# Loading 80 of 128 partitions of the queries and keys, and values in one run a partition, in an attention kernel with two MLPs

## The chip, the cores and the metric

The kernel runs on one core of a Trainium2 chip. The metric is the device time of one execution in microseconds (us); less is better. The kernel before was run three times.

## What is computed

A causal block attention (4 batches, 8 heads, 576 positions, 64 values a head; all in float32), then two MLPs on the 2304 tokens of width 512, each with a hidden width of 2048.

```
def _attn_ref(q, k, v):
    scores = scale * np.matmul(q, k.transpose(0, 1, 3, 2))
    mask = block_i >= block_j                # blocks of 64 positions
    scores = np.where(mask, scores, -1000000000.0)
    attn = np.exp(scores - max); attn = attn / (sum + 1e-09)
    return np.matmul(attn, v)
...
    x = attn_out.transpose(0, 2, 1, 3).reshape(B * S, H * D)
    x = (np.maximum(x @ w_in, 0.0) ** 2) @ w_out             # first MLP
    return rational(x @ w_in2, a, b) @ w_out2                 # second MLP
```

## The kernel before

The work goes through three stages on the same engines. In the first one attention is computed head by head, and half of the first MLP's hidden units (`moe_a`) are woven between. Then come the other half of the first MLP (`yb`, `hb`) and the second MLP (`hc`, `yc`). In all of them TensorE multiplies, ScalarE (ACT) and VectorE (DVE) empty the accumulators, and GpSimd (POOL) does element-wise work from memory on chip.

Attention is done in *visits* (`Visit`, L172). Heads 0 to 7 are visited twice: visits 0 to 7 do the tiles 0 to 2 of their rows (`gis == (0, 1)`), visits 8 to 15 the tiles 3 and 4. From head 8 on one visit does a whole head. A visit consists of *slots*, and a slot i goes through the following chain: the scores S on TensorE (`emit_s`, L294, tiles `sy`, `sx`); the row maxima on DVE (`emit_max`, L315, `stat`); the exponentials with their sums on ACT (`emit_exp`, L328, tile `p`); transposes on TensorE (`emit_t`, L370, `tp`) and their copies into `pt_plain` by ACT (L388); the product with the values on TensorE (`emit_pv`, L429, `pv`), with the inverse sums spread by POOL (L344, `rb`), transposed (L436, `rows`), copied by ACT (L437, `xp`) and multiplied in by DVE (L438, `xp`). POOL turns the result into the operand `xt` of the first MLP (L451, L452), and a DMA stores it (L453).

Heads 0 to 9 are *plain* (`PLAIN = 10`): the scores are one product in float32. The host stacks the operand so that its first 64 partitions hold the head's 64 values, the next five hold marks that add the mask, and the other 59 hold zeros:

```
        out[:, 0:d_, pad:] = xt
        out[PLAIN:, d_:P, pad:] = xt[PLAIN:]
        for t in range(5):
            out[0:PLAIN, d_ + t, P * t:P * t + d_] = mark
```

Queries and keys are loaded by DMA with all 128 partitions (`load_qk`, L181, tiles `qr`, `kr`, two buffers under each of two tags in the first visits), and POOL scales the queries in place (`prep_qk`, L228), except those of visit 0. The values of two plain heads share one tile of 5 blocks of 128 columns, 64 of them for each head (`load_v`, L210), so that a load lands in pieces of 64 values. The heads 10 to 31 split both operands into two parts and need all 128 partitions; `make_two` (L200) copies partitions 64 to 127 of head 9's operands into constants for them.

Between all this, eight weight tiles `w_ai` of `moe_a` are converted (`Converter`, L81): a DMA loads `raw_ai` (512 KB, L93, three buffers), ACT and DVE make `cv_ai` of it (L117, and L118, L119, L121, L122), and the next call rounds it (ACT, L110) and subtracts (POOL, L111) into `w_ai`.

No order is written out by hand: the program lists the work, and a scheduler that estimates the duration of each instruction and transfer fixes one order for each engine when the kernel is built. On the chip an engine takes its instructions in this order, and each waits for what it needs. Scores have few accumulators (`sx` and `sy` one each, `mm` two), so a slot's scores wait until the exponentials four slots before have been read out. All of SP's transfers are issued in one order too, and at most eight are under way.

Of the kernel before, what the change touches and what calls it, by code (L numbers as in the profile page):

```python
# [8 lines left out]
F32 = mybir.dt.float32  # L9
# [8 lines left out]
P = 128  # L18
S = 576
SP = 640  # L20
D = 64
# [6 lines left out]
NB = 12  # L28
SCALE = 0.125
PLAIN = 10  # L30
SUBS = ((0, 320), (320, S))
SUB = 320
BLK = 512
# [11 lines left out]
def f(ap):  # L45
    return ap.bitcast(F32)
# [3 lines left out]
def attention_moe_moe(ctx: ExitStack, tc: tile.TileContext, q, k, v, wi1, wo1, wi2, wo2, a, b, out):  # L50
    nc = tc.nc
# [24 lines left out]
        name=nc.get_next_instruction_name(), act_func_set_id=EXP_LN_SET, ins=[], outs=[]))  # L76
# [59 lines left out]
    attn = tc.alloc_tile_pool(name="attn", bufs=1)  # L136
# [35 lines left out]
    class Visit:  # L172
        def __init__(self, n, hd, at, gis):
            self.n, self.hd, self.plain, self.at, self.gis = n, hd, hd < PLAIN, at, gis

            self.scale = SCALE if n == 0 else 1.0

            self.q0, self.q1 = (0, 3 * P) if gis == (0, 1) else (3 * P, SP) if gis == (2, 3) else (0, SP)
            self.k1 = SUB if gis == (0, 1) else S

    def load_qk(un, eng=nc.sync):  # L181
        if len(un.gis) == 2 and un.n % 4 > 1:

            un.qr = f(attn.tile([P, SP], F32R, tag="qh", name=f"qr{un.n}", bufs=2))
            un.kr = f(attn.tile([P, S], F32R, tag="kk", name=f"kr{un.n}", bufs=2))
        else:
            un.qr = attn.tile([P, SP], F32, tag="qr", name=f"qr{un.n}", bufs=2)
            un.kr = attn.tile([P, S], F32, tag="kr", name=f"kr{un.n}", bufs=2)

        cuts = ((0, 256, 0, 192), (256, un.q1, 192, un.k1)) if un.n == 0 else ((un.q0, un.q1, 0, un.k1),)  # L190
        for q0, q1, k0, k1 in cuts:
            nc.sync.dma_start(un.qr[:, q0:q1], q[un.hd][:, q0:q1])
            eng.dma_start(un.kr[:, k0:k1], k[un.hd][:, k0:k1])

# [13 lines left out]
    def load_v(un):  # L210
        src = v[un.hd].rearrange("p (c d) -> p c d", d=D)
        if un.plain:
            if un.hd % 2 == 0:
                un.vs = attn.tile([P, 5, P], F32, tag="vs", name=f"vs{un.n}", bufs=2)
            else:
                un.vs = units[un.n - 1].vs
            o = D * (un.hd % 2)
            nv = 3 if un.gis == (0, 1) else 5
            nc.sync.dma_start(un.vs[:, 0:nv, o:o + D], src[:, 0:nv])
        else:  # L220
            un.vr = attn.tile([P, 5, D], F32, tag="vr", name=f"vr{un.hd}", bufs=1)
            nc.sync.dma_start(un.vr, src)

    def prep_qk(un, step):
        if un.plain:
            if step == 0 and un.scale == 1.0:
                cols = un.qr[:, un.q0:un.q1]
                nc.gpsimd.tensor_scalar(cols, cols, SCALE, 0.0, op0=ALU.mult, op1=ALU.add)  # L228
            return
        if step == 0:  # L230
            hd = un.hd
            un.qh = attn.tile([P, SP], F32R, tag="qh", name=f"qh{hd}", bufs=2)
            un.kk = attn.tile([P, S], F32R, tag="kk", name=f"kk{hd}", bufs=2)
            nc.scalar.activation(un.qh, un.qr, AF.Copy, scale=SCALE)
            nc.scalar.activation(un.kk, un.kr, AF.Copy)
        else:
            un.q2, un.k2 = q_two[un.hd % 2], k_two[un.hd % 2]
            nc.vector.scalar_tensor_tensor(
                un.q2[0:D], un.qr[0:D], SCALE, f(un.qh[0:D]), op0=ALU.mult, op1=ALU.subtract)
            nc.gpsimd.tensor_tensor(un.kk[D:P], un.kr[D:P], f(un.kk[D:P]), op=ALU.subtract)  # L240
            nc.sync.dma_start(f(un.k2[0:D]), f(un.kk[0:D]))
# [24 lines left out]
    def emit_s(i):  # L266
        un, gi = slots[i]
        g = GROUPS[gi]

        upper = un.gis == (0, 1)  # L270
        if un.hd % 2 and gi == 0 if upper else gi % 2:
            ps = ps1.tile([P, 2, 512], F32, tag="sx", name=f"sx{i}")
            if gi != 3:
                ps = ps[:, 0, :]
        else:
            tag = "mm" if upper and gi == 1 else "sy"
            ps = ps1.tile([P, 512], F32, tag=tag, name=f"sy{i}", bufs=BANKS[tag])
        spsum[i] = ps
        for t in g:

            cols = slice(P * t, P * (t + 1))
            if un.plain:
                products = [(un.qr[:, cols], un.kr)]
            else:
                products = [(un.qh[:, cols], un.kk), (un.q2[:, cols], un.k2)]
            w_ = P * t + D
            if t == 4:
                parts = [(ps[:, 0, 0:HS], 0, HS), (ps[:, 1, 0:HS], HS, S)]
            else:
                o = D if t == 1 else 0  # L290
                parts = [(ps[:, o:o + w_], 0, w_)]
            for dst, lo, hi in parts:
                for z, (lhs, rhs) in enumerate(products):
                    last = nc.tensor.matmul(dst, lhs, rhs[:, lo:hi], start=z == 0, stop=z == len(products) - 1)  # L294
        marks.append(last)
# [62 lines left out]
    def emit_t(i):  # L358
        nonlocal pt
        un, gi = slots[i]  # L360
        g = GROUPS[gi]
        if un.hd == PLAIN and gi == 0:
            pt = attn.tile([P, 2, 3, SP], F32R, tag="pt", name="pt", bufs=1)
# [48 lines left out]
    def emit_pv(un, half):  # L412
        hd = un.hd
        b_, h = divmod(hd, H)
        hp, odd = divmod(h, 2)
        first, end = SUBS[half]
        n = end - first

        if un.plain and not odd:
            return  # L420
        if un.plain or not odd:
            xpair[hp, half] = attn.tile([P, SUB], F32, tag="xp", name=f"xp{hd}_{half}", bufs=3)
        xp = xpair[hp, half]
        ps = ps1.tile([P, 512], F32, tag="tp", name=f"pv{hd}_{half}", bufs=3)
        lo, hi = (0, D) if odd else (D, 0)
        if un.plain:
            for i, (c, src, dst, width) in enumerate(PV[half]):
                for n_, o in enumerate((0, D)):
                    nc.tensor.matmul(ps[o:o + D, dst:dst + width], un.vs[:, c, o:o + D],  # L429
                                     un.pt[:, n_, ROW[c], src:src + width],  # L430
                                     start=i == 0, stop=i == len(PV[half]) - 1)
            rb = spread.pop((hd, half))
            rows = ps1.tile([P, 512], F32, tag="tp", name=f"rows{hd}_{half}", bufs=3)
            lead = D if half == 0 else 0
            for at in range(rb.shape[1]):
                nc.tensor.transpose(rows[:, P * at:P * (at + 1)], rb[:, at], ident)  # L436
            nc.scalar.activation(xp[:, 0:n], rows[:, lead:lead + n], AF.Copy)  # L437
            nc.vector.tensor_tensor(xp[:, 0:n], ps[:, 0:n], xp[:, 0:n], op=ALU.mult)  # L438
        else:
            mm = [(z, *m) for z in range(2) for m in PV[half]]  # L440
            for i, (z, c, src, dst, width) in enumerate(mm):
                nc.tensor.matmul(ps[:, dst:dst + width], un.vs[:, c, :], un.pt[:, z, ROW[c], src:src + width],
                                 start=i == 0, stop=i == len(mm) - 1)
            tmp = attn.tile([P, SUB], F32, tag="tmp", name=f"tmp{hd}_{half}", bufs=2)
            nc.scalar.activation(tmp[hi:hi + D, 0:n], ps[lo:lo + D, 0:n], AF.Copy)
            nc.vector.tensor_tensor(xp[hi:hi + D, 0:n], ps[hi:hi + D, 0:n], tmp[hi:hi + D, 0:n], op=ALU.add)
        if odd:
            if b_ not in xtile:
                xtile[b_] = xpool.tile([P, 2, KK, S], F32R, tag="xt", name=f"xt{b_}", bufs=2)
            xh, xl = (xtile[b_][:, z, hp, first:end] for z in range(2))  # L450
            nc.gpsimd.tensor_scalar(xh, xp[:, 0:n], 1.0, 0.0, op0=ALU.mult, op1=ALU.add)  # L451
            nc.gpsimd.tensor_tensor(xl, xp[:, 0:n], f(xh), op=ALU.subtract)  # L452
            nc.sync.dma_start(xs[:, hp, S * b_ + first:S * b_ + end], xp[:, 0:n])  # L453
# [9 lines left out]
    def moe_a(b_):  # L463
# [9 lines left out]
        xt = xtile[b_]  # L473
        for s, (first, end) in enumerate(SUBS):
            n = end - first
# [102 lines left out]
    for i in range(NI + 5):  # L578
# [15 lines left out]
        if 0 <= i - 4 < NI:  # L594
            un, gi = slots[i - 4]
# [4 lines left out]
        advance(steps(i + 1) - steps(i + 0.5), gate)  # L600
        if i == 4 * PLAIN - 4:
            late = make_two(slots[i][0])
# [118 lines left out]
    for u in range(len(units) + LAG):  # L721
        if u < len(units):
# [7 lines left out]
            ps = h_matmul(wB["i", m], xt[j], n, f"b{j}_{m}")  # L730
# [40 lines left out]
    for u in range(len(units) + LAG):  # L771
# [16 lines left out]
        if u < len(units):  # L788
# [7 lines left out]
            ps = h_matmul(w3["i", m], xt[j], n, f"c{j}_{m}")  # L796
# [9 lines left out]
        if u >= LAG:  # L806
# [3 lines left out]
            for c in range(n // P):  # L810
# [7 lines left out]
                if m == NM - 1:  # L818
                    if c % 2 == 0:
                        o = g2.tile([P, 2, DM], F32, tag="wraw", name=f"o{j}_{c}", bufs=2)  # L820
# [64 lines left out]
```

## Time and profile before

| | us |
|---|---|
| three runs: lowest, median, highest | 1018.55, 1020.74, 1020.98 |
| profiled execution, whole | 1018.61 |
| its span, first to last instruction | 1016.8 |
| TensorE busy in the span | 995.1 (98%) |
| VectorE, ScalarE, GpSimd busy | 741.8, 728.5, 591.1 |
| DMA queue of SP: share of the 16 DMA engines | 32.7% |

The profile shows one execution. 1018.61 less 1016.8 leaves 1.8 us around the span. A matmul's end is modelled, so TensorE's busy time includes some waiting; its starts are measured.

### The profile page before, as it was taken

What the parts mean: (1) busy time and instruction counts of PE and PEld (TensorE: products, weight loads), DVE (VectorE), ACT (ScalarE), POOL (GpSimd) and SP (SyncE); (2) the same over time, 40 slices, a digit from 0 to 9 for tenths busy, and PEclk for the clock granted to TensorE, in tenths of its full rate; (3) what the DMA queues carried; (4) which work ended last, traced back from release to release, by engine and by line L of the source; (5) the groups of instructions that cost most, each with busy time, mean ns of one, the idle gap of its engine ahead of it and who ended that gap; (6) DMA issues with size and microseconds to landing.
All of it is one profiled execution on the core that took longest, in us unless ns stands there. A gap on an engine that the chain in (4) does not pass through costs nothing. (4 is left out here: it accounts for less than half of the span.)

```text
span 1016.8 us, 17069 instructions
## 1 busy us (share of the span) xinstructions
PE 995.1 (98%) x5721; PEld 882.6 (87%) x5721; DVE 741.8 (73%) x1412; ACT 728.5 (72%) x1620; POOL 591.1 (58%) x632
## 2 busy tenths in 40 slices
PE   7999999999999999999999999999999999999997
PEld 5678998999999999999888888887888888899996
DVE  6799688768787756676676756887766766777766
ACT  6789697768787746664555557887787776787775
POOL 4767686868786845630232448767556554655552
PEclk9999999999999999999999999999999999999999
DMA  8866435243332204567656572001101100100000
GB/s 268 253 195 216 128 97 154 88 114 116 119 93 81 67 24 141 191 193 256 231 166 200 172 242 88 1 1 42 41 1 32 42 1 1 57 17 1 32 1 31
DMA packets 63894, 106.58 MB, mean 105 GB/s; under 512 B 16064, under 2 KB 34496, under 8 KB 63808
## 3 DMA queue, kind: packets, MB, share of 16 engines
q1 hardware_dynamic: 63520, 105.34, 32.7%
q8 instruction: 45, 0.74, 0.3%
q14 instruction: 41, 0.34, 0.1%
q10 hardware_dynamic: 288, 0.16, 0.1%
HBM read 79.17 MB, written 23.07 MB: 101 GB/s over the span
## 5 line engine op out<-in xcount | busy, mean ns | idle before, releaser
L816 PE MATMUL yc<-w_co,gc 128*128 128x512 f32 x864 | 211.6, 391 | 2.9 <-ACT gc L776 2.9
L707 PE MATMUL hc<-xc,w_ci 128*128 128x512 f32 (+1 forms) x960 | 211.2, 368 | 0.0
L707 PEld LDWEIGHTS hc<-xc,w_ci 128*128 128x128 f32 x960 | 176.1, 188 | 26.3
L816 PEld LDWEIGHTS yc<-w_co,gc 128*128 128x128 f32 x864 | 161.2, 188 | 35.5 <-ACT gc L776 4.4
L777 POOL TENSOR_TENSOR gc<-t,gc 128x512 fp32r<-128x512 f32 (+1 forms) x78 | 105.1, 1353 | 126.1 <-issue 103.2
L482 PE MATMUL ha<-xt,w_ai 128*128 128x320 f32 (+1 forms) x768 | 122.5, 305 | 0.5 <-POOL xt L451 0.5
L495 PE MATMUL ya<-ga,w_ao 128*128 128x320 f32 (+1 forms) x768 | 116.8, 299 | 1.6 <-ACT r L508 0.9
L802 POOL TENSOR_TENSOR wq<-wq,ab 128x512 f32<-128x512 f32 (+1 forms) x78 | 96.3, 1235 | 28.6 <-ACT wq L800 28.6
L482 PEld LDWEIGHTS ha<-xt,w_ai 128*128 128x128 f32 x768 | 107.6, 189 | 5.1 <-issue 3.0
L495 PEld LDWEIGHTS ya<-ga,w_ao 128*128 128x128 f32 x768 | 106.5, 189 | 3.5 <-ACT r L508 1.1
L747 PE MATMUL yb<-gb,w_bo 128*128 128x512 f32 (+1 forms) x480 | 106.0, 368 | 0.0
L707 PE MATMUL hb<-xb,w_bi 128*128 128x512 f32 (+1 forms) x480 | 105.7, 368 | 0.0
L776 ACT ACTIVATE gc<-t 128x512 fp32r<-128x512 f32 (+1 forms) x80 | 47.1, 589 | 73.0 <-DVE t L785 72.9
L803 DVE TENSOR_TENSOR t<-hc,t 128x512 f32<-128x512 f32 (+1 forms) x80 | 50.9, 637 | 66.1 <-ACT t L801 66.1
L747 PEld LDWEIGHTS yb<-gb,w_bo 128*128 128x128 f32 x480 | 87.6, 188 | 12.0 <-DVE yp L752 0.3
L707 PEld LDWEIGHTS hb<-xb,w_bi 128*128 128x128 f32 x480 | 87.4, 188 | 11.3 <-ACT yo L500 0.2
L356 POOL TENSOR_SCALAR p<-p,stat 64x64 f32<-64x64 f32 (+4 forms) x110 | 64.4, 586 | 44.2 <-DVE stat L352 11.1
L402 DVE TENSOR_TENSOR pt<-tp,pt 128x128 fp32r<-128x128 f32 (+2 forms) x176 | 63.2, 391 | 27.0 <-ACT pt L400 16.6
L783 DVE SCALAR_TENSOR_TENSOR wq<-wq,ab 128x512 f32<-128x512 f32 (+1 forms) x80 | 54.9, 687 | 33.5 <-ACT ab L782 22.2
L370 PE MATMUL tp<-ident,p 128*128 128x128 f32 x480 | 77.8, 278 | 0.5 <-ACT xp L437 0.3
L400 ACT ACTIVATE pt<-tp 128x128 fp32r<-128x128 f32 (+2 forms) x176 | 57.1, 362 | 26.6 <-PE tp L370 25.0
L785 DVE SCALAR_TENSOR_TENSOR t<-t,coef,ab 128x512 f32<-128x512 f32 (+1 forms) x80 | 66.8, 835 | 1.7
(137 smaller groups left out, 2004.8 us busy)
## 6 DMA issues: line engine op xcount, KB each, us to landing
kr<-in_k_dram SPq DMA_DIRECT2D x32, 288.0 KB, 3.6
raw_ci<-in_wi_dram SPq DMA_DIRECT2D x16, 512.0 KB, 4.1
raw_co<-in_wo_dram SPq DMA_DIRECT2D x16, 512.0 KB, 3.9
qr<-in_q_dram SPq DMA_DIRECT2D x24, 320.0 KB, 3.3
raw_ai<-in_wi_dram SPq DMA_DIRECT2D x8, 512.0 KB, 5.1
raw_ao<-in_wo_dram SPq DMA_DIRECT2D x8, 512.0 KB, 4.0
raw_bi<-in_wi_dram SPq DMA_DIRECT2D x8, 512.0 KB, 3.4
raw_bo<-in_wo_dram SPq DMA_DIRECT2D x8, 512.0 KB, 3.5
```

The source lines that it names most:

```text
L356: nc.gpsimd.tensor_scalar(pv, pv, st[r:P, 6 + n:7 + n], 0.0, op0=ALU.mult, op1=ALU.add)
L370: nc.tensor.transpose(ps[:, P * n:P * (n + 1)], ptile(slots[i][0], t)[:, P * c:P * (c + 1)], ident)
L400: nc.scalar.activation(high, src, AF.Copy)
L402: nc.vector.tensor_tensor(low, src, f(high), op=ALU.subtract)
L482: nc.tensor.matmul(ps[:, 0:n], w[:, zw, P * kk:P * (kk + 1)], xt[:, zx, kk, first:end], start=i == 0, stop=i == 3 * KK - 1)
L495: nc.tensor.matmul(ps[:, 0:n], wA["o", m][:, zw, P * c:P * (c + 1)], gs[m][:, zg, 0:n], start=i == 0, stop=i == 3 * HALF - 1)
L707: nc.tensor.matmul(ps[:, 0:n], w[:, zw, P * kk:P * (kk + 1)], xt[:, zx, kk, 0:n], start=i == 0, stop=i == 3 * KK - 1)
L747: nc.tensor.matmul(acc[j, c][:, 0:n], wB["o", m][:, zw, P * c:P * (c + 1)], g[:, zg, 0:n], start=m == 0 and i == 0, stop=last and i == 2)
L777: (nc.vector if u - 2 >= len(units) - END else nc.gpsimd).tensor_tensor(g[:, 1, 0:n], t, f(g[:, 0, 0:n]), op=ALU.subtract)
L785: nc.vector.scalar_tensor_tensor(t, t, a0, r, op0=ALU.add, op1=ALU.mult)
L802: (nc.vector if u >= len(units) - END else nc.gpsimd).tensor_tensor(w, w, ab, op=ALU.mult)
L816: last = nc.tensor.matmul(acc[j, c], g[:, zg, P * c:P * (c + 1)], w3["o", m][:, zw, :], start=m == 0 and i == 0, stop=m == NM - 1 and i == 2)
```

## The change

There are two edits. For heads 0 to 8 (17 visits) `load_qk`, the scaling on POOL and the scores' operands are cut to partitions 0 to 79 (`un.kp`); head 9, whose upper partitions become constants, keeps 128. The tile of a pair's values is laid out head by head, so that a load writes one run of 3 or 5 times 64 values in each partition.

```
+KPLAIN = 80
+            self.kp = KPLAIN if hd < PLAIN - 1 else P
...
-            nc.sync.dma_start(un.qr[:, q0:q1], q[un.hd][:, q0:q1])
-            eng.dma_start(un.kr[:, k0:k1], k[un.hd][:, k0:k1])
+            nc.sync.dma_start(un.qr[0:un.kp, q0:q1], q[un.hd][0:un.kp, q0:q1])
+            eng.dma_start(un.kr[0:un.kp, k0:k1], k[un.hd][0:un.kp, k0:k1])
...
-                un.vs = attn.tile([P, 5, P], F32, tag="vs", name=f"vs{un.n}", bufs=2)
+                un.vs = attn.tile([P, 2, 5, D], F32, tag="vs", name=f"vs{un.n}", bufs=2)
             else:
                 un.vs = units[un.n - 1].vs
-            o = D * (un.hd % 2)
             nv = 3 if un.gis == (0, 1) else 5
-            nc.sync.dma_start(un.vs[:, 0:nv, o:o + D], src[:, 0:nv])
+            nc.sync.dma_start(un.vs[:, un.hd % 2, 0:nv], src[:, 0:nv])
...
-                cols = un.qr[:, un.q0:un.q1]
+                cols = un.qr[0:un.kp, un.q0:un.q1]
...
-                products = [(un.qr[:, cols], un.kr)]
+                products = [(un.qr[0:un.kp, cols], un.kr[0:un.kp])]
...
-                    nc.tensor.matmul(ps[o:o + D, dst:dst + width], un.vs[:, c, o:o + D],
+                    nc.tensor.matmul(ps[o:o + D, dst:dst + width], un.vs[:, n_, c],
```

The loads now look shorter to the scheduler, and it fixes other orders. On TensorE, ACT and DVE they differ from the start up to the scores of visit 9 (`sy18`) and are the same from there to the end of the kernel; on POOL and SP single instructions still move up to about the loads of head 9. In the rows that follow, the number behind a name is that of the slot (`sx10`, `tp6`), of the visit (`qr7`), of the odd head of a pair with its half (`rb3_1`) or of the converted weight tile (`cv_ai2`).

GpSimd before, around the scaling of visit 7's queries:

```order
L451 TENSOR_SCALAR xt0_299<-xp1_0_285 128x320
L344 TENSOR_SCALAR rb3_1_319<-sums1_139 128x128 x3
L228 TENSOR_SCALAR qr7_309<-qr7_309 128x384
L452 TENSOR_TENSOR xt0_299<-xp1_0_285,xt0_299 128x320
L111 TENSOR_TENSOR w_ai1_349<-cv_ai1_273,w_ai1_349 128x512
L228 TENSOR_SCALAR qr8_343<-qr8_343 128x256
```

GpSimd now, at the same place:

```order
L112 TENSOR_TENSOR w_ai0_270<-cv_ai0_214,w_ai0_270 128x512
L229 TENSOR_SCALAR qr7_309<-qr7_309 80x384
L345 TENSOR_SCALAR rb3_1_319<-sums1_139 128x128 x3
L112 TENSOR_TENSOR w_ai1_349<-cv_ai1_273,w_ai1_349 128x512
L229 TENSOR_SCALAR qr8_343<-qr8_343 80x256
L452 TENSOR_SCALAR xt0_299<-xp1_0_285 128x320
```

`qr7` has moved ahead of the first `xt` and of `rb3`.

VectorE before, around the maxima of slot 10:

```order
L118 TENSOR_SCALAR raw_ai2_166<-raw_ai2_166 128x512
L121 TENSOR_SCALAR cv_ai1_273<-cv_ai1_273 128x512
L315 TENSOR_REDUCE stat2_124<-sx10_360 64x1
L315 TENSOR_REDUCE stat2_124<-sx10_360 128x1
L340 TENSOR_SCALAR sums1_139<-sums1_139 128x2x3
L119 SCALAR_TENSOR_TENSOR raw_ai2_166<-raw_ai2_166 128x512
L122 SCALAR_TENSOR_TENSOR cv_ai1_273<-cv_ai1_273,raw_ai1_158 128x512
L438 TENSOR_TENSOR xp1_0_285<-pv1_0_286,xp1_0_285 128x320
```

VectorE now:

```order
L119 TENSOR_SCALAR raw_ai2_166<-raw_ai2_166 128x512
L120 SCALAR_TENSOR_TENSOR raw_ai2_166<-raw_ai2_166 128x512
L439 TENSOR_TENSOR xp1_0_285<-pv1_0_286,xp1_0_285 128x320
L122 TENSOR_SCALAR cv_ai2_352<-cv_ai2_352 128x512
L123 SCALAR_TENSOR_TENSOR cv_ai2_352<-cv_ai2_352,raw_ai2_166 128x512
L316 TENSOR_REDUCE stat2_124<-sx10_360 64x1
L316 TENSOR_REDUCE stat2_124<-sx10_360 128x1
```

The maxima of `sx10` have moved behind the multiplication of `xp1` and behind both steps of `cv_ai2`.

ScalarE before, around the copies of the transposes of slots 6 and 7:

```order
L328 ACTIVATE p2_2_111,sums0_138<-sy11_373,stat3_125 128x320
L388 ACTIVATE pt_plain_121<-tp6_0_337 128x192
L388 ACTIVATE pt_plain_121<-tp6_0_337 128x128
L388 ACTIVATE pt_plain_121<-tp7_0_367 128x3x128
L328 ACTIVATE p3_1_98,sums1_139<-sy12_405,stat4_126 64x64
L328 ACTIVATE p3_1_98,sums1_139<-sy12_405,stat4_126 128x192
L328 ACTIVATE p4_1_100,sums1_139<-sy13_424,stat5_127 128x320
L110 ACTIVATE w_ai2_440<-cv_ai2_352 128x512
```

ScalarE now:

```order
L329 ACTIVATE p3_1_98,sums1_139<-sy12_405,stat4_126 64x64
L329 ACTIVATE p3_1_98,sums1_139<-sy12_405,stat4_126 128x192
L389 ACTIVATE pt_plain_121<-tp5_0_327 128x3x128
L329 ACTIVATE p4_1_100,sums1_139<-sy13_424,stat5_127 128x320
L111 ACTIVATE w_ai2_440<-cv_ai2_352 128x512
L118 ACTIVATE cv_ai3_443<-raw_ai3_220 128x512
L389 ACTIVATE pt_plain_121<-tp6_0_337 128x192
L389 ACTIVATE pt_plain_121<-tp6_0_337 128x128
L389 ACTIVATE pt_plain_121<-tp7_0_367 128x3x128
```

Four pieces of work (the exponentials of `sy12` and of `sy13`, `w_ai2`, `cv_ai3`) now come ahead of the copies of `tp6` and `tp7`. On TensorE the scores `sy16` have moved ahead of the product `pv3` that uses these copies.

## Rows read from the trace of the kernel before

**Rows 1.** The page: busy time of each engine, and the slices of TensorE.

```profile
PE 995.1 (98%) x5721; PEld 882.6 (87%) x5721; DVE 741.8 (73%) x1412; ACT 728.5 (72%) x1620; POOL 591.1 (58%) x632
...
PE   7999999999999999999999999999999999999997
```

**Rows 2.** Stretches (us from the span's start): length, busy time of each engine, clock, DMA.

```profile
core 0: us, PE busy (x) PEld busy (x) DVE busy (x) ACT busy (x) POOL busy (x), PEclk, DMA share, GB/s
5.00:10.00 5.00, 3.63 (x10) 2.23 (x10) 2.18 (x8) 1.83 (x9) 1.02 (x2) 1.00 1.01 349
...
11.00:20.00 9.00, 8.47 (x51) 6.29 (x49) 6.81 (x18) 7.55 (x28) 4.85 (x8) 1.00 0.94 269
...
20.00:30.00 10.00, 8.47 (x47) 5.54 (x48) 9.82 (x23) 8.17 (x30) 7.04 (x12) 1.00 0.98 310
...
41.00:80.00 39.00, 38.86 (x234) 28.49 (x234) 35.98 (x62) 32.17 (x94) 26.98 (x32) 1.00 0.74 217
```

**Rows 3.** What TensorE waited for from 0 to 50 us: total, times, longest.

```profile
PE sy L294 <- DMA kr<-in_k_dram: 3.6, 1, 3.6
PE sx L294 <- DMA kr<-in_k_dram: 1.4, 1, 1.4
PE sx L294 <- POOL qr L228: 1.2, 1, 1.2
```

**Rows 4.** Transposes on TensorE, 9.6 to 11.1 us, then 12 to 13 us.

```profile
L370 PE MATMUL tp<-ident,p 128*128 128x128 f32 x7 | 1.7, 421 | 0.0
...
L370 PE MATMUL tp<-ident,p 128*128 128x128 f32 x5 | 0.7, 272 | 0.0
```

**Rows 5.** DMA issues: size of each, median us from issue to landing.

```profile
qr<-in_q_dram SPq DMA_DIRECT2D x7, 192.0 KB, 4.2
...
vs<-in_v_dram SPq DMA_DIRECT2D x8, 96.0 KB, 4.2
...
kr<-in_k_dram ACTq DMA_DIRECT2D x1, 96.0 KB, 2.7
...
kr<-in_k_dram ACTq DMA_DIRECT2D x1, 64.0 KB, 2.6
```

**Rows 6.** Timeline of TensorE, 20 to 30 us: start, length, what, idle before.

```profile
22.64 0.75 PE L429 MATMUL pv<-pt_plain,vs 128*64 128x320 f32 x2 [0.18 <-DVE xp L438]
...
24.60 0.82 PE L294 MATMUL sx<-kr,qr 128*128 128x64 f32 x4 [1.22 <-POOL qr L228]
...
28.17 1.02 PE L294 MATMUL sy<-kr,qr 128*128 128x448 f32 x2
```

**Rows 7.** Timeline of ScalarE, 21 to 30 us.

```profile
21.88 0.31 ACT L328 ACTIVATE p<-sx,stat 64x64 f32<-64x64 f32 x1
...
24.63 0.31 ACT L328 ACTIVATE p<-sy,stat 64x64 f32<-64x64 f32 x1
...
25.45 0.52 ACT L328 ACTIVATE p<-sy,stat 128x320 f32<-128x320 f32 x1
...
26.13 0.63 ACT L110 ACTIVATE w_ai<-cv_ai 128x512 fp32r<-128x512 f32 x1
...
28.76 0.31 ACT L328 ACTIVATE p<-sx,stat 64x64 f32<-64x64 f32 x1 [1.67 <-DVE stat L315]
...
29.58 0.68 ACT L117 ACTIVATE cv_ai<-raw_ai 128x512 f32<-128x512 f32 x1
```

**Rows 8.** Timeline of VectorE, 20 to 25 us: maxima of slot 10, then the pieces now ahead.

```profile
20.31 0.60 DVE L315 TENSOR_REDUCE stat<-sx 64x1 f32<-64x64 f32 x2
...
21.49 0.68 DVE L122 SCALAR_TENSOR_TENSOR cv_ai<-cv_ai,raw_ai 128x512 uint32<-128x512 uint32 x1
22.10 0.48 DVE L438 TENSOR_TENSOR xp<-pv,xp 128x320 f32<-128x320 f32 x1
...
22.96 0.44 DVE L121 TENSOR_SCALAR cv_ai<-cv_ai 128x512 f32<-128x512 f32 x1
```

**Rows 9.** All that uses `kr`, 0 to 130 us: length, PE, PEld, ACT, POOL.

```profile
0.00:130.00 130.00, 36.99 (x120) 20.19 (x120) 4.12 (x6) 5.74 (x4) 1.00 0.69 209
```

## The prediction, made before the changed kernel was run

> **What bounds the kernel now.** I read the page first, then the busy times by stretch, then TensorE's waits, and last the timelines around the waits. TensorE is busy for 995.1 of 1016.8 us, and of the 40 slices only the first and the last are below 9 tenths [rows 1]. From 41 to 80 us it is busy for 38.86 of 39.00 us [rows 2]; there and later its order is the same before and after. So the change can win or lose time almost only up to the scores of visit 9, before 41 us, and what it wins there moves the whole rest of the kernel forward.
>
> In this beginning TensorE waits three times in a way that the edits touch: 3.6 us for the first keys and queries, 1.4 us for visit 1's keys, 1.2 us for GpSimd's scaling of visit 7's queries [rows 3]. It is no bound there by itself: from 20 to 30 us VectorE is busy for 9.82 of 10.00 us, ScalarE for 8.17 and GpSimd for 7.04 [rows 2]. The 16 DMA engines are full (shares of 0.94 to 1.01 from 5 to 30 us) [rows 2], but that matters only where an engine waits for a landing. From 41 us on TensorE itself is the bound.
>
> **What is removed.**
>
> a) The first wait, 3.6 us [rows 3]. The first two loads shrink from 128 and 96 KB to 80 and 60 KB. On ScalarE's queue 96 KB took 2.7 us to land and 64 KB took 2.6 us [rows 5], so most of a landing doesn't go with size. Bounds: 0, and 3/8 of 2.7 = 1.0 us. I take the end near the two rows: -0.2 us.
>
> b) The wait for visit 1's keys, 1.4 us [rows 3]. Up to and including them, 192 + 160 + 192 + 160 = 704 KB are asked for; 5/8 of that is 440 KB. The 264 KB (0.27 MB) saved are worth 0.8 us at the 349 GB/s of that stretch [rows 2]. Bounds 0 and 1.4; I take -0.8 us.
>
> [...]
>
> c) Between 11 and 20 us TensorE is idle for 9.00 - 8.47 = 0.5 us [rows 2], around the first `rows1` and the scores of visit 3, which both stand behind `rb1` on GpSimd. Now `qr3` comes ahead of `rb1`. Bounds 0 and 0.5; I take -0.5 us.
>
> d) The wait for `qr7`. Its GpSimd row moves ahead of `xt` and `rb3`, so the idle 1.22 us before `sx14`, and 0.18 us before `pv3`, lose their cause [rows 6]. Bounds 0 and the whole idle time from 20 to 30 us, 10.00 - 8.47 = 1.5 us [rows 2]; I take -1.4 us.
>
> Together -2.9 us, with a most of 1.0 + 1.4 + 0.5 + 1.5 = 4.4 us.
>
> **What the edits cost elsewhere.** The values' loads become 768 or 1280 bytes a partition. Those of 96 KB took 4.2 us to land, against 2.7 us for as many bytes of keys [rows 5], so each may gain up to 1.5 us; but nothing waits for values in TensorE's list [rows 3]. I take 0; without this cover it would be a gain again.
>
> The scores now contract over 80 partitions. All instructions that use `kr` keep TensorE busy for 36.99 us [rows 9], and every one that I saw has 128 partitions. Bounds: 0, and 3/8 of 36.99 us in 17 of 18 visits, -13.1 us. The nearest row is the same matmul with the same columns, so I take 0. [...] The scaling of 80 partitions on GpSimd is taken as unchanged too: GpSimd's 5.74 us on all that uses `kr` [rows 9] is the most that could be in question, and of its waits only d is on the path.
>
> **What is added.** The new order puts conversion work ahead of attention work, on engines that take their rows strictly in order.
>
> e) VectorE and `sx14`. `sx14` needs the accumulator of `sx10`, so the exponentials of `sx10` must be over. VectorE took `sx10`'s maxima at 20.31 us, before `xp1` (22.10 us) [rows 8]; now they come behind `xp1` and both steps of `cv_ai2`. With a to c won, `xp1` would start at 22.10 - 1.5 = 20.6 us; adding 0.48 + 0.44 + 0.68 us [rows 8] the maxima start at 22.2 and end at 22.8 us, where the exponentials had started at 21.88 us [rows 7]. These last some 0.8 us (as those of slot 12, 24.63 to 25.45 us [rows 7]), so `sx14` starts at 23.6 us. It should have been 24.60 - 2.9 = 21.7 us. So +1.9 us: d is given back, and a part of a to c. Behind the waiting maxima on VectorE stand those of slots 11 to 13, for which ScalarE waits. Bounds 0 (`xp1` earlier by the same 1.9 us) and 1.9 + 1.0, if `cv_ai2` on ScalarE comes late too.
>
> f) ScalarE and `pv3`. Ahead of the copies of `tp6` and `tp7`, which `pv3` needs, now stand the exponentials of slot 12 (24.63 to 25.45: 0.82 us) and slot 13 (to 26.13: 0.68 us), `w_ai2` (0.63 us) and `cv_ai3` (0.68 us) [rows 7]: 2.8 us. TensorE has as cover the scores `sy16` (1.02 us) and the first product of `pv3` (0.75 us) [rows 6], which have moved behind `sx14`. 2.8 - 1.8 = +1.0 us. Bounds 0 (ScalarE's idle 1.67 us before slot 14's exponentials [rows 7] takes it up) and 2.8 us.
>
> **The sum.** -0.2 - 0.8 - 0.5 - 1.4 + 1.9 + 1.0 = 0.0 us. The profiled execution would again take 1018.6 us (span 1016.8 and 1.8 around it). It lies 2.1 us below the median 1020.74 us. The four known times lie in two pairs (1018.55 and 1018.61; 1020.74 and 1020.98), and a median of new runs may fall into either, so I predict their mean: 1019.7 us. A difference of less than 0.3% (3.1 us) from the median can't be told from none.
>
> **Rivals.**
>
> Faster (22%): the DVE and ACT moves are covered and a to d stay. For it: ScalarE is idle for 1.67 us in front of `sx14`'s exponentials [rows 7], and GpSimd and ScalarE have room from 20 to 30 us [rows 2]. Against it: VectorE has 0.18 us of room there. 1019.7 - 2.9 = 1016.8 us, with the most of a to d 1015.3 us; against the median 1020.74 us both are over 0.3%.
>
> The number of partitions sets a matmul's time (3%): up to 13.1 us less, 1006.6 us. Only the absence of a row speaks for it.
>
> Slower (13%): one mechanism, the alternation of VectorE and ScalarE. Wherever a conversion step now stands ahead of a maximum, VectorE waits for ScalarE's half of the conversion, and ScalarE then for the maximum. Its price is the one such wait in the profile, 1.67 us [rows 7]; with `cv_ai1` to `cv_ai4` four times, 6.7 us, against the 1.5 us of a to c that remain: +5.2 us, 1024.9 us. It decides once the mean of the four exceeds (1.5 + 4.1)/4 = 1.4 us (4.1 us being the way from 1019.7 us to 0.3% above the median). VectorE at 9.82 of 10.00 us speaks for it; that the four steps are hardly ever late together speaks against.
>
> The loads don't get shorter (5%): 80 partitions spread worse over the DMA engines, or the landing doesn't go with bytes. a and b go: 1019.7 + 1.0 = 1020.7 us. The small slope of the two rows in a speaks for it, the full queues against.
>
> **How the numbers follow.** My forecast, gains given back in the new order, has 57%, its own range from 1017.7 to 1022.0 us (half of e and f absent, or at their upper bounds). Faster: 22 + 3 = 25%. Same: 57 + 5 = 62%. Slower: 13%. The range for 8 in 10 goes from 1016.2 us (1019.7 - 2.9 - 0.6 of the further 1.5) to 1023.0 us (e at 2.9 and f at 2.8 with only a to c kept would be +3.0 to +4.2; the lower of these on 1019.7, rounded).
>
> **What would show it.** a: the first scores start near 3.4 us instead of 3.6. b: visit 1's scores start 1 us earlier, and the last transpose of 421 ns ends at 11 us or before. c, d: no wait for `qr` in TensorE's list, and `qr7` scaled before 22 us. e: the exponentials of slot 10 later than 21.88 us although the scores are earlier. f: TensorE idle before `pv3`, released by ScalarE's copies. The sum: the first matmul of `moe_a` (`ha`) starts where it does before, within 2 us. If it starts 3 us earlier, the faster rival is right, and e and f were wrong; 4 us later, the slower one. If the means of the scores' matmuls change at equal columns, the zero for the contraction was wrong.

## The result, and the profile after

The changed kernel takes 1026.13 us (median of 6 runs, 1025.45 to 1031.64), against 1019.82 us for the kernel before (6 runs beside it, 1018.46 to 1020.98). The ratio is 1.007, with a 95% interval from 1.0051 to 1.009: it is slower, by more than the 0.3% that can be told apart. The prediction said 1019.7 us, and gave slower 13%. The profiled execution took 1025.92 us.

Over the whole span TensorE is as busy as in [rows 1]; the page of the changed kernel:

```profile
PE 1002.2 (98%) x5721; PEld 886.7 (87%) x5721; DVE 746.7 (73%) x1412; ACT 728.7 (71%) x1620; POOL 590.1 (58%) x632
```

The stretches of [rows 2], after the change (same columns):

```profile
5.00:10.00 5.00, 5.00 (x19) 4.30 (x18) 3.47 (x12) 4.10 (x16) 0.51 (x1) 1.00 1.03 317
11.00:20.00 9.00, 9.00 (x31) 6.04 (x30) 6.49 (x15) 5.89 (x23) 4.84 (x9) 1.00 0.81 216
20.00:30.00 10.00, 8.33 (x40) 5.42 (x37) 7.13 (x15) 6.44 (x22) 6.50 (x13) 0.94 0.68 222
41.00:80.00 39.00, 38.40 (x225) 26.52 (x224) 35.43 (x59) 32.64 (x94) 23.83 (x28) 1.00 0.58 184
```

From 11 to 20 us TensorE is busy all the time and yet issues 31 matmuls where it had issued 51. From 20 to 30 us VectorE falls from 9.82 to 7.13 us and ScalarE from 8.17 to 6.44: both now wait. Transposes in three windows, 7 to 12.5 us, 12.5 to 22 us and 24 to 25.2 us, to be read against [rows 4]:

```profile
L371 PE MATMUL tp<-ident,p 128*128 128x128 f32 x12 | 3.0, 421 | 0.0
...
L371 PE MATMUL tp<-ident,p 128*128 128x128 f32 x3 | 0.8, 419 | 0.0
...
L371 PE MATMUL tp<-ident,p 128*128 128x128 f32 x9 | 1.1, 273 | 0.0
```

Up to 22 us they still take some 420 ns; before, they took 272 ns from 12 us on. The trace also keeps the times at which the granted clock changed: its first entry, here called the rise, gives a granted share of 1.0, the upper level, from 22.0 us on, and from 11.7 us on in the trace of before. From 28.8 to 32.2 us the entry is 0.5, the lower level. The clock column of the stretches stands at 1.00 ahead of the first entry too, so there the level is read from the transposes (some 420 ns at the lower, 272 ns at the upper). What TensorE waited for from 0 to 50 us, against [rows 3]:

```profile
PE sy L295 <- DMA kr<-in_k_dram: 3.1, 1, 3.1
PE sx L295 <- issue: 0.9, 1, 0.9
PE sy L295 <- issue: 0.8, 1, 0.8
```

The waits for visit 1's keys (1.4 us) and for visit 7's queries (1.2 us) are gone. Two new ones stand in the timeline of TensorE, against [rows 6]: `sx14`, `sy16`, the first product of `pv3`, and then the scores of visit 9 and the first `ha`:

```profile
26.19 0.79 PE L295 MATMUL sx<-kr,qr 80*128 80x64 f32 x4 [0.87 <-issue]
26.81 0.70 PE L295 MATMUL sy<-kr,qr 80*128 80x320 f32 x2
28.31 1.36 PE L295 MATMUL sy<-kr,qr 80*128 80x448 f32 x2 [0.80 <-issue]
29.59 1.33 PE L430 MATMUL pv<-pt_plain,vs 128*64 128x320 f32 x2
...
40.59 1.02 PE L295 MATMUL sy<-kr,qr 80*128 80x448 f32 x2
...
46.49 0.96 PE L483 MATMUL ha<-xt,w_ai 128*128 128x320 f32 x3
```

The scores of visit 9 had started at 36.04 us and `ha` at 41.91: the beginning has become 4.6 us longer. What `sx14` waits for is seen on VectorE, against [rows 8]:

```profile
16.87 0.43 DVE L122 TENSOR_SCALAR cv_ai<-cv_ai 128x512 f32<-128x512 f32 x1 [1.11 <-ACT cv_ai L118]
...
21.49 0.49 DVE L439 TENSOR_TENSOR xp<-pv,xp 128x320 f32<-128x320 f32 x1 [0.47 <-PE pv L430]
21.90 1.69 DVE L122 TENSOR_SCALAR cv_ai<-cv_ai 128x512 f32<-128x512 f32 x1
23.63 0.81 DVE L123 SCALAR_TENSOR_TENSOR cv_ai<-cv_ai,raw_ai 128x512 uint32<-128x512 uint32 x1
24.47 0.60 DVE L316 TENSOR_REDUCE stat<-sx 64x1 f32<-64x64 f32 x2
...
30.20 1.54 DVE L122 TENSOR_SCALAR cv_ai<-cv_ai 128x512 f32<-128x512 f32 x1 [1.48 <-ACT cv_ai L118]
```

and on ScalarE, against [rows 7] (exponentials of slots 8, 10 and 12):

```profile
18.96 0.31 ACT L329 ACTIVATE p<-sy,stat 64x64 f32<-64x64 f32 x1 [1.62 <-DVE stat L316]
...
25.16 0.31 ACT L329 ACTIVATE p<-sx,stat 64x64 f32<-64x64 f32 x1 [2.47 <-DVE stat L316]
...
27.28 0.31 ACT L329 ACTIVATE p<-sy,stat 64x64 f32<-64x64 f32 x1 [0.69 <-DVE sums L342]
```

In turn VectorE waits for ScalarE's half of a conversion (1.11, 1.48 us) and ScalarE for VectorE's maxima (1.62, 2.47 us). That is the alternation that the slower rival describes.

### The profile page after: what moved, and what is told of

Its sections match the earlier page's. It is cut to its first block, busy times and chain, and to the rows that moved or that the text cites. A ratio compares the mean times of both kernels' runs of the same rounds, so it can differ in the third digit from the quotient of the medians.

```text
span 1024.1 us, 17081 instructions
## 1 busy us (share of the span) xinstructions
PE 1002.2 (98%) x5721; PEld 886.7 (87%) x5721; DVE 746.7 (73%) x1412; ACT 728.7 (71%) x1620; POOL 590.1 (58%) x632
## 4 chain that ended last, share of the span: by engine, by line
PE 74%; DVE 9%; ACT 6%; DMA 5%; issue 3%; POOL 3%; SPq 0%; ACTq 0%; DVEq 0%; POOLq 0%
PE yc L817 15%; PE hc L708 15%; PE yb L748 7%; PE ya L496 7%; PE ha L483 7%; PE hb L708 6%; PE tp L371 4%; PE pv L443 4%; PE sy L295 3%; PE sx L295 3%; PE pv L430 2%; DMA raw_ci<-in_wi_dram 1%; DVE ab L785 1%; DMA raw_bo<-in_wo_dram 1%; DVE t L786 1%
```

## The experiments

Three causes were weighed. **A**: the 80-row matmuls keep TensorE's clock low, and that is the loss. **B**, later **C**: the new order is the loss, through the conversion steps ahead of the maxima. **D**: the new order of TensorE, GpSimd and SP takes part in the loss. The ratios stand against runs of the kernel before on the same chip beside each experiment. Clock up, `sx14` and visit 9 (us) are those of the one profiled execution; the first is the rise in the trace's entries. After the rise and up to 50 us the clock fell back in the changed kernel, E3, E4, E5, E7, E9, E12, E14, E15 and E17, in each case for some us between 24 and 36 us (in E17 also from 10.0 to 13.4 us), and not in the others.

| | ratio (95%) | median us | clock up | `sx14` | visit 9 |
|---|---|---|---|---|---|
| before | 1 | 1019.82 | 11.7 | 24.60 | 36.04 |
| changed | 1.0070 (1.0051 to 1.0090) | 1026.13 | 22.0 | 26.19 | 40.59 |
| E1 | 0.9997 (0.9982 to 1.0011) | 1019.81 | 11.9 | 23.65 | 35.39 |
| E2 | 0.9991 (0.9981 to 1.0001) | 1020.10 | 11.7 | 22.51 | 34.64 |
| E3 | 1.0059 (1.0036 to 1.0083) | 1026.82 | 21.8 | 26.53 | 42.03 |
| E4 | 1.0006 (0.9993 to 1.0019) | 1022.05 | 13.2 | 23.44 | 37.71 |
| E5 | 1.0051 (1.0032 to 1.0071) | 1026.93 | 11.9 | 26.80 | 41.20 |
| E6 | 1.0055 (1.0031 to 1.0078) | 1025.70 | 21.2 | 25.46 | 40.24 |
| E7 | 1.0013 (0.9992 to 1.0035) | 1021.85 | 15.2 | 24.31 | 36.44 |
| E8 | 1.0121 (1.0077 to 1.0165) | 1034.25 | 41.1 | 34.45 | 48.99 |
| E9 | 1.0070 (1.0058 to 1.0083) | 1028.34 | 11.5 | 27.09 | 42.78 |
| E10 | 0.9991 (0.9974 to 1.0008) | 1019.84 | 9.7 | 22.73 | 34.17 |
| E11 | 1.0027 (1.0008 to 1.0046) | 1024.04 | 14.3 | 23.25 | 35.11 |
| E12 | 1.0019 (1.0004 to 1.0033) | 1022.78 | 15.3 | 23.34 | 38.45 |
| E13 | 1.0035 (1.0016 to 1.0055) | 1023.12 | 24.0 | 26.87 | 41.73 |
| E14 | 1.0043 (1.0023 to 1.0063) | 1024.08 | 19.9 | 25.47 | 40.45 |
| E15 | 1.0044 (1.0025 to 1.0063) | 1025.34 | 7.7 | 24.28 | 39.28 |
| E16 | 1.0036 (1.0017 to 1.0054) | 1024.18 | 7.5 | 24.52 | 37.73 |
| E17 | 1.0041 (1.0024 to 1.0059) | 1023.73 | 6.6 | 24.46 | 40.75 |
| E18 | 1.0005 (0.9993 to 1.0016) | 1020.42 | 8.3 | 22.82 | 36.34 |

**The parts of the change.** E1 is the kernel before with 80 rows in the score matmuls alone:

```
-                products = [(un.qr[:, cols], un.kr)]
+                kp = 80 if un.hd < PLAIN - 1 else P
+                products = [(un.qr[0:kp, cols], un.kr[0:kp])]
```

> Only the score matmuls of the first nine heads contract over 80 rows; loads, scaling and values are as in the kernel before. Theory A (the 80-row matmuls keep TensorE's granted clock at its lower level): transposes at 421 ns and the clock record at 0.5 until well past 20 us instead of about 11.2, span about 5 us longer, time 1023 to 1026 us. Theory B (the different order and waits of the first 30 us do it): this kernel loads as before did, so its clock rises at 11 to 12 us and its time is before's, 1018.5 to 1021 us.

E2 has the values' layout alone (`KPLAIN = 128` in the changed kernel).

> Only the values' layout in one run a partition; queries, keys and matmuls on 128 partitions. Both theories A and B: the clock rises at about 11 us as before and the time is before's within 0.3%, 1017 to 1022 us. If the layout of the values took part in the loss, it is above 1023 us.

E3 has the 80 partitions alone, with the old `load_v` and `emit_pv`.

> Only the 80 partitions, in loads, scaling and matmuls; values as before. Theories A and B alike: the loss of the changed kernel is here whole, clock up at about 22 us, 1024.5 to 1027.5 us. If the values' layout carries part of it (the sync queue's order), 1021 to 1024 us.

E4 has 80 partitions only from visit 8 on (`if hd < PLAIN - 1 and n >= 8`).

> 80 partitions only from the ninth visit on (the first eight visits' queries, keys and matmuls stay on 128); the values' layout as in the changed kernel. Theory A: the clock rises at about 11 us as before, and once it is up the 80-row matmuls later either leave it (time 1017.5 to 1021.5 us) or drop it while visits of 80 rows follow each other (0.5 in the record between 20 and 45 us, 1022 to 1027 us). Theory B: order and early loads of before, so clock and time of before, 1017.5 to 1021.5 us.

The layout of the values does nothing (E2), and the 80 partitions carry the loss (E3). In E4 the later visits show no loss in the runs, so it comes from visits 0 to 7. (Its median, 1022.05 us, lies just above the 1021.5 us that both theories gave, and its clock fell back from 30.3 to 33.7 us, as A allowed; against the runs beside it the ratio is still 1.0006.) E1 refuted A as it stood: the matmuls had 80 rows and the clock rose at 11.9 us. But the order of E1 is nearly that of before.

**Rows against order.** In E5 to E7 each engine's first 50 to 80 instructions are chained in a given order (`ORDER` holds the built order of the other kernel), with no new wait:

```
+    traced = {i.name: i for i in nc.cur_bb.bb.instructions}
+    for names in ORDER.values():
+        names = names.split()
+        for p_, c_ in zip(names, names[1:]):
+            tc.add_manual_dep(
+                traced["I-" + c_], "I-" + p_,
+                mybir.DependencyInfo(mybir.DependencyClass.NoSync, mybir.DependencyReason.DATA), reason="order")
```

E5: the kernel before in the changed order.

> The kernel before (loads, scaling and score matmuls on 128 partitions, old layout of the values), with each engine's instructions pinned to the changed kernel's order. Theory A now reads: what keeps the granted clock at its lower level is 80-row score matmuls standing for most of the first 20 us, with fewer transposes and value products between them than in the order of before. By A the clock rises at 12 us or before here (the matmuls have all 128 rows), the waits of sx14 and sy16 behind VectorE and ScalarE remain, and the time is 1018 to 1022 us. Theory B (the order alone): rise at about 22 us and 1024 to 1028 us, as the changed kernel.

E6: E5 with the edit of E1.

> The kernel of E5 with one thing more: the score matmuls of the first nine heads contract over 80 of the 128 loaded rows. Theory A: the rise moves from about 12 us to about 22 us and the time to 1024 to 1028 us. Theory B: no difference from E5, both at 1024 to 1028 us. If neither shows the late rise, it is the shorter loads (the earlier start) that bring it.

E7: the changed kernel in the order of before.

> The changed kernel (80 partitions in loads, scaling and matmuls, new layout of the values), pinned to the order of before. Theory B: no stall at sx14 and sy16, clock up at about 11 us, a gain of 0.5 to 2 us from the earlier start: 1017 to 1020 us. Theory A: 80-row matmuls as in E1, where the clock still rose at 11.9 us, but begun earlier; if the rise stays at 12 us the time is as in theory B, if the earlier scores push it to 15 us or more, 1021 to 1025 us.

E8: E1 with `kp = 64`.

> The kernel of E1 with the contraction of the first nine heads cut to 64 rows; this leaves the mask out of their scores. Loads and order are those of E1. Theory A: with still fewer rows the clock no longer rises at 11.9 us, as it did with 80 rows, but 3 us or more later, transposes at 421 ns past 14 us, time 1021 to 1027 us. Theory B: order as in E1, so rise at 11.9 us and 1018.5 to 1021 us.

E5 has all 128 rows, and its clock rises at 11.9 us, as A expected, but it keeps the loss. E6 rises at 21.2 us, as A expected, and loses no more than E5. E7 loses nothing that can be told from none, though B's rise at 11 us and 1020 us at most were missed (15.2 us, 1021.85 us). So the order carries the time, while the rise moved with the rows (11.9 us with 128 in E5, 21.2 with 80 in E6, one execution each). E8 (1034.25 us, where A allowed 1027 at most) shows how late it came with 64: with loads and order of E1, transposes from 12 to 36 us, and TensorE in the same stretch:

```profile
L371 PE MATMUL tp<-ident,p 128*128 128x128 f32 x17 | 4.9, 436 | 0.0
```

```profile
12.00:36.00 24.00, 24.00 (x69) 13.90 (x69) 11.99 (x31) 12.95 (x47) 9.12 (x17) 1.00 0.64 190
```

TensorE is busy for 24.00 of 24.00 us, at the lower level throughout (the rise is the entry at 41.1 us). In an order near that of before E8 loses 1.2%.

**The early clock in the changed order.** E9 is the changed kernel in its own order, with the loaded rows of visits 0 to 7 padded to 128:

```
+    qz = [early.tile([P, 3 * P], F32, name=f"qz{n}") for n in range(4)]
+    kz = [early.tile([P, SUB], F32, name=f"kz{n}") for n in range(4)]
+    for t in qz + kz:
+        nc.vector.memset(t[0:P - KPLAIN], 0.0)
...
+            to, kp = (slice(P - KPLAIN, P), KPLAIN) if un.n < 8 else (slice(0, un.kp), un.kp)
+            nc.sync.dma_start(un.qr[to, q0:q1], q[un.hd][0:kp, q0:q1])
```

> The changed kernel in its own order, with one thing more: in visits 0 to 7 the 80 loaded rows land in partitions 48 to 127 of tiles whose other 48 partitions are zeroed once at the start, and scores contract over all 128. Loads, starts and order are the changed kernel's; only the rows that the matmul runs over differ. Theory A (80 rows keep the granted clock low): transposes drop to 272 ns by 12 us at the latest instead of 22, the waits of sx14 and sy16 behind VectorE and ScalarE stay or grow, and a drop of the clock after them may stay; time 1019 to 1023 us. Theory B (the order alone): rise at 22 us, 1024 to 1028 us as the changed kernel.

E10: the same, in the order of before.

> The same padded contraction with the short loads, pinned to the order of before. Both theories hold that nothing of the loss is left. By A the clock rises by 12 us and the earlier start (a, b) is kept: 1016.5 to 1019.5 us; if the wait of sx14 for the scaling of visit 7's queries (1.2 us in before) grows and lets the clock drop as in E7, 1019 to 1022 us. By B it equals E7, 1019 to 1023 us.

E11: E1 with `kp = 72`.

> E1 with a contraction over 72 rows, which still takes in every row that holds data; loads and order those of E1. Theory A: between E1 (80 rows, rise at 11.9 us, 1019.8 us) and E8 (64 rows, rise at 41.1 us, 1034 us): rise between 15 and 41 us, 1021 to 1033 us. If E8's loss came from the missing mask and not from the rows, E1's 11.9 us and 1018.5 to 1021 us.

E12: the changed kernel with `KPLAIN = 96`.

> The changed kernel with 96 instead of 80 partitions in loads, scaling and matmuls; the order is the one that comes out of it, near to the changed kernel's. Theory A: the clock rises by 12 to 15 us instead of 22; what the order costs remains; 1018.5 to 1023 us. Theory B: 1023 to 1027 us, rise at about 22 us.

E9 spoke against A. Its transposes at 11.5 to 13 us, its stretch from 20 to 30 us, and `sx14`:

```profile
L388 PE MATMUL tp<-ident,p 128*128 128x128 f32 x6 | 0.8, 273 | 0.0
```

```profile
20.00:30.00 10.00, 4.99 (x24) 3.22 (x23) 7.97 (x17) 6.45 (x25) 7.03 (x11) 0.93 0.72 223
```

```profile
27.09 0.79 PE L312 MATMUL sx<-kz,qz 128*128 128x64 f32 x4 [2.93 <-POOL xt L470]
```

The clock is up ten us earlier than in the changed kernel (11.5 against 22.0 us), and TensorE only waits more: from 20 to 30 us it is busy for 4.99 us instead of 8.33. (`xt` on GpSimd is named as the releaser since it ended last; ScalarE's row below says what `sx14` waits for.) VectorE and ScalarE of E9:

```profile
18.21 0.43 DVE L131 TENSOR_SCALAR cv_ai<-cv_ai 128x512 f32<-128x512 f32 x1 [2.60 <-ACT cv_ai L127]
...
25.37 0.60 DVE L333 TENSOR_REDUCE stat<-sx 64x1 f32<-64x64 f32 x2
```

```profile
26.07 0.31 ACT L346 ACTIVATE p<-sx,stat 64x64 f32<-64x64 f32 x1 [2.50 <-DVE stat L333]
```

They wait for each other as long as in the changed kernel or longer. E9 alone doesn't settle A, since its clock falls back, from 28.5 to 35.3 us. But four pairs of kernels with the same order differ in the rows of the score matmuls (the padded ones also in their tiles) and in the rise: E5 and E6, E9 and the changed kernel, and below E15 and E13, E16 and E14. Their ratios lie within 0.1 points of each other, also in E16, where the clock was up from 7.5 us on and did not fall back. E10 shows the same data in the order of before: no loss. E11, which leaves nothing out, speaks for the rows and against the missing mask as the cause in E8: it loses 0.27%. Its runs lie from 1018.9 to 1027.9 us, and the profiled one (1018.9) shows the rise at 14.3 us, just below the 15 that A gave; when the clock rose in the others was not seen. E12 fits A's range (rise at 15.3 us), but its order is another again, so it tells little apart.

**Which rows of the order.** E13 moves rows of VectorE in the changed kernel's pinned order (the number is the slot's or the weight tile's):

```
-max7 cv_ai1 sums1 cv_ai1 sums1 max8 max9 raw_ai2 xp1 cv_ai2 cv_ai2 max10 max11
+max7 sums1 sums1 max8 max9 cv_ai1 cv_ai1 raw_ai2 max10 max11 xp1 cv_ai2 cv_ai2
```

> The changed kernel in its own order but for VectorE: cv_ai1's two steps move behind the maxima of slots 8 and 9, and the maxima of slots 10 and 11 ahead of xp1 and of cv_ai2's two steps. Theory C (the order: conversion steps that wait for ScalarE stand ahead of maxima, and ScalarE then waits for these): sx14's wait of 0.87 us and most of sy16's 0.80 us go, the scores of visit 9 start 1 to 2 us earlier than the changed kernel's 40.6 us, 1023.5 to 1025.5 us; no more than that, since TensorE is late there from its low clock too. Theory A (the late rise of the clock carries the loss): 1025 to 1027.5 us.

E14 adds ScalarE:

```
-exp12 copy_tp5 exp13 w_ai2 cv_ai3 copy_tp6 copy_tp7
+copy_tp5 copy_tp6 copy_tp7 exp12 exp13 w_ai2 cv_ai3
```

> E13 and on ScalarE the copies of slots 6 and 7's transposes ahead of the exponentials of slots 12 and 13, w_ai2 and cv_ai3. Theory C: pv3 no longer waits for the copies; visit 9's scores at 37.5 to 39.5 us, 1021.5 to 1024.5 us. Theory A: 1024.5 to 1027.5 us.

E15 is E9 with the edit of E13.

> The kernel of E9 (padded to 128 rows, the changed kernel's order, clock up at 11.5 us) with VectorE's moves of E13. Theory C: sx14 starts at 23 to 25 us instead of 27.1, visit 9's scores at 37.5 to 40 us instead of 42.8, 1021 to 1025 us. If C is wrong and another of the moved rows holds sx14 back, 1026 to 1029 us as E9.

E16 is E9 with both.

> E15 with ScalarE's move of E14 too. Theory C: nearly all of the loss is gone, visit 9's scores at 35.5 to 38 us, 1019 to 1022.5 us. If C is wrong, 1025 to 1029 us.

E17 is E9 with VectorE and ScalarE wholly in the order of before.

> The padded kernel (clock up early) with VectorE's and ScalarE's whole order of before; TensorE, GpSimd and SP in the changed order. E9, all engines in the changed order, took 1028.3 us, and E10, all in that of before, 1019.8 us. Theory C (the alternation of VectorE and ScalarE carries the loss): 1019 to 1022 us, visit 9's scores at 34 to 37 us. Theory D (GpSimd's and TensorE's new order carries what E16 left): 1023 to 1026 us, visit 9's scores past 37 us.

E18 is E17 with TensorE in the order of before too.

> E17 with TensorE in the order of before too; only GpSimd and SP are left in the changed order. Theory C: as E17, 1019 to 1022 us. Theory D splits here: if TensorE's order (sx14 and sy16 ahead of pv3) carries the rest, 1019 to 1021.5 us and 2 us or more below E17; if GpSimd's and SP's carry it, within 1 us of E17.

E13 was below its range in the median: with these rows of VectorE moved the ratio is 1.0035 instead of 1.0070 (the intervals just overlap). `sx14` then starts with no wait before it:

```profile
26.87 0.71 PE L304 MATMUL sx<-kr,qr 80*128 80x64 f32 x4
```

Its profile missed the expectation of an earlier visit 9 (41.73 us); in that execution the clock came up only at 24.0 us, which may be why. `sy16`'s wait, most of which was to go by C, stayed: 0.99 us in E13 and 1.47 us in E14, by the profile for ScalarE's exponentials. E14's copies brought nothing that can be told from E13; its median lies in C's range, its visit 9 (40.45 us) doesn't. With the clock early, E15 and E16 brought `sx14` from 27.09 to 24.28 and 24.52 us and visit 9 to 39.28 and 37.73 us, as C expected, but not the time of E16 (that of E15 lies 0.3 us above its range). In E16's profiled execution only 1.7 of the 6.1 us that its span (1022.9 us) is longer than that of before lie ahead of visit 9; the others come later, as described at the end of the next section. E17 speaks for a second cause in the order: even the whole order of before on these two engines leaves 0.4% in the runs, so C is only a part. TensorE in E17 and in E18, from `sx14` on:

```profile
24.46 0.79 PE L312 MATMUL sx<-kz,qz 128*128 128x64 f32 x4 [0.61 <-POOL rb L362]
...
27.67 1.86 PE L312 MATMUL sy<-kr,qr 80*128 80x448 f32 x2 [1.43 <-POOL qr L246]
29.46 1.33 PE L447 MATMUL pv<-pt_plain,vs 128*64 128x320 f32 x2
...
40.75 1.02 PE L312 MATMUL sy<-kr,qr 80*128 80x448 f32 x2
```

```profile
22.14 0.75 PE L447 MATMUL pv<-pt_plain,vs 128*64 128x320 f32 x2
22.82 0.82 PE L312 MATMUL sx<-kz,qz 128*128 128x64 f32 x4
...
26.41 0.92 PE L312 MATMUL sy<-kr,qr 80*128 80x448 f32 x2
...
36.34 1.02 PE L312 MATMUL sy<-kr,qr 80*128 80x448 f32 x2
```

In E17 the first product of `pv3` stands behind `sx14` and `sy16`, which wait (`sy16` for the scaling of visit 8's queries on GpSimd, which has the changed order in both); in E18 it is done before them. So the 0.79 points between E9 and E10 fall in three steps: VectorE and ScalarE 0.29 (E9 to E17), TensorE 0.36 (E17 to E18), GpSimd and SP 0.14 points (E18 to E10). The last can't be told from none; the steps' intervals are about 0.2 wide on each side. The shares hold for swapping the engines in this turn; another turn was not tried. TensorE's share includes the clock: in the profiled execution of E17 it fell back from 27.0 to 33.9 us, while `sy16` waited and after, and in E18 it stayed up there.

## Why the prediction was wrong, point by point

- **a, b** happened and were larger than said: the first scores start at 3.08 instead of 3.58 us, and visit 1's follow at 5.34 instead of 7.43 us without a wait, 2.1 us and not 1.0.
- **c, d** happened as causes: no wait for `qr` is left.
- **The clock.** The sum took a and b whole, -1.0 us, and left out that the rise could come later. The zero for the contraction over 80 rows was the author's estimate; no row of before shows a contraction over 80. For a matmul's time at one level it was right; 320 columns at the upper level took 432 ns in E1 with 80 rows and in E9 with 128:

```profile
L295 PE MATMUL sy<-kr,qr 80*128 80x320 f32 x3 | 1.1, 432 | 0.0
```

```profile
L312 PE MATMUL sy<-kz,qz 128*128 128x320 f32 x2 | 0.7, 432 | 0.0
```

But the rise came 10 us later (22.0 against 11.7 us), and TensorE gave back what a to c had won: slot 10's scores start at 22.0 instead of 17.9 us. In this order that is not what the loss hangs on, for E9 with the earlier rise is as slow, and so it is in the other three pairs above.

- **e** is the step that failed first, by size. The maxima of slot 10 were to start at 22.2 us and started at 24.47. Of these 2.3 us, 0.9 are `xp1` (21.49 against 20.6 us, behind `pv1` at the lower clock, where 320 columns of `pv` took 768 ns from 14 to 22 us, and 458 ns before from 17 to 24 us), 1.25 the step of `cv_ai2` (1.69 us instead of the 0.44 us of [rows 8]), and 0.1 the next one (0.81 against 0.68). `sx14` started at 26.19 instead of 23.6 us. The term took each step at its length in the old order, and `xp1` at the upper level; it was priced by one row in one place, though the same alternation of VectorE and ScalarE stood at `cv_ai1` and `cv_ai3` as well (1.11 and 1.48 us).
- **f** failed in its cover. `sy16` and the first product of `pv3` were counted as work that hides ScalarE's copies. Both stand behind `sx14` now, and so wait with it: `sy16` for another 0.80 us, behind slot 12's exponentials. TensorE's own new order, which the sum counted only as this cover, was a cost. Moving the copies themselves (E14) brought nothing that can be told; TensorE's order is worth 0.36 points (E17 to E18).
- **The slower rival** (13%, 1024.9 us) named a part of the mechanism, and the prediction's own sign for it was right: `ha` starts 4.6 us later (4 us was the mark). Its price of 6.7 us for four waits of one kind is the sum 1.11 + 1.62 + 2.47 + 1.48 = 6.7 us of waits of both engines in the rows above; they lie partly beside other work, and TensorE's order, which it left out, took a share as large (E18), so that the two sums agree is luck. VectorE at 9.82 of 10.00 us should have raised its chance.
- **The ranges.** Three bounds don't follow from the words beside them: half of e and f absent is -1.45 us, 1018.3 and not 1017.7 us, and both at their upper bounds, 2.9 and 2.8, are +2.8 us, 1022.5 and not 1022.0 us. Of the two sums for 8 in 10, only +4.2 us comes out of e, f and a to c (1023.9 us). The measured median lies above all of them.
- Of the 7.3 us between the two spans (1024.1 and 1016.8), 4.6 lie before visit 9. The other 2.7 us lie later, 2.4 of them in two waits between 400 and 520 us of the profiled execution, which the profile before had not:

```profile
PE yb L748 <- DVE yp L753: 1.4, 1, 1.4
PE hb L708 <- ACT yo L501: 1.0, 1, 1.0
```

They come in some executions of kernels in either order (E10 has both, E1 one, E3 none). What starts them stays open. In E10's profiled execution they and others eat more than it wins in the beginning: visit 9 starts at 34.17 us, 1.9 us earlier than before, and the span is still 1019.0 us. So one profiled execution shows the beginning better than the whole, and the ratios of the runs decide.

No version was measurably faster than before; E10 and E2, both at 0.9991, come nearest.

## What to carry to other kernels

When an edit changes sizes that a scheduler sees, price the new order first: list each row that moved ahead of another engine's input, and count every such place, not only the first. Work moved behind an instruction that may wait is no cover for that wait. Before crediting a wait that goes, ask which engine is late next: here a TensorE with the clock up at 11.5 instead of 22.0 us (E9) only waited longer: from 20 to 30 us it was busy for 4.99 instead of 8.33 us.

## What the runs showed of the hardware

**The granted clock and the rows of a contraction.** All times of a rise are those of one execution of each kernel. With equal loads and equal order on TensorE, the rise came at 11.9 us with 80 rows (E1), at 14.3 with 72 (E11) and at 41.1 with 64 (E8); in the changed order at 11.9 with 128 (E5) and at 21.2 with 80 (E6). In E6 from 11 us (9.00 of 9.00 us up to 20 us), in E8 from 12 us (24.00 of 24.00 up to 36 us) and in the changed kernel from 6 us (16.00 of 16.00 up to 22 us) up to the rise TensorE had been working without a gap. In some executions the clock fell back after waits, as in the changed kernel from 28.8 to 32.2 us, after the 0.87 and 0.80 us above; in E13 it did not, after 0.99 us. What sets the level was not shown.

**VectorE's conversion step beside GpSimd.** `cv_ai1`'s first step took 0.43 us at 16.87 us, with GpSimd idle up to 17.78; `cv_ai2`'s took 1.69 us at 21.90, and `cv_ai3`'s 1.54 at 30.20, beside these rows of GpSimd:

```profile
17.78 0.72 POOL L229 TENSOR_SCALAR qr<-qr 80x384 f32<-80x384 f32 x1 [2.97 <-DMA qr<-in_q_dram]
...
21.67 1.26 POOL L112 TENSOR_TENSOR w_ai<-cv_ai,w_ai 128x512 fp32r<-128x512 f32 x1
22.91 0.40 POOL L229 TENSOR_SCALAR qr<-qr 80x256 f32<-80x256 f32 x1
...
30.19 1.26 POOL L112 TENSOR_TENSOR w_ai<-cv_ai,w_ai 128x512 fp32r<-128x512 f32 x1
```

The step at 21.90 us took 1.69 - 0.43 = 1.26 us more than the one at 16.87, and `w_ai` beside it still had 1.03 us to run; GpSimd's spans are rough. Why the step is longer there was not shown. No run moved GpSimd's rows alone, but E13 moved VectorE's against them, and the long step changed places. There `cv_ai1`'s takes 1.82 us, and `cv_ai2`'s, as GpSimd's `w_ai` ends, 0.42 us. VectorE and GpSimd of E13:

```profile
20.73 1.82 DVE L131 TENSOR_SCALAR cv_ai<-cv_ai 128x512 f32<-128x512 f32 x1
...
25.99 0.42 DVE L131 TENSOR_SCALAR cv_ai<-cv_ai 128x512 f32<-128x512 f32 x1
```

```profile
21.00 1.26 POOL L121 TENSOR_TENSOR w_ai<-cv_ai,w_ai 128x512 fp32r<-128x512 f32 x1
...
24.79 1.26 POOL L121 TENSOR_TENSOR w_ai<-cv_ai,w_ai 128x512 fp32r<-128x512 f32 x1
```
